# A pre-LN block of linear attention and spatial-gating MLP: earlier warm-up, head statistics on ScalarE, x loads held back, a split last tile, and a new instruction order

## The chip, the cores and the metric

One core of one Trainium2 chip. The metric is the device time of one execution in microseconds (us). Before the prediction the kernel had three unprofiled runs: median 236.93 us (236.36 to 237.14). PE is the tensor engine, VectorE is DVE in the profile, ScalarE is ACT, Pool is GpSimd, and SP is the engine that issues most of the DMAs.

## The reference, cut to what matters

Sequence S = 2048, width D = 512, half width Fh = 896, all in bf16.

```python
x = A_x
h  = x + _A_ref(_layernorm(x), A_wqkv, A_wo)                    # linear attention, 32 heads
h2 = h + _B_ref(_layernorm(h), B_w_in, B_w_sp, B_b_sp, B_w_out)

# _B_ref, cut:
z  = _gelu(x @ w_in)                       # 2048 x 1792
z1 = z[..., :Fh]
z2 = _layernorm(z[..., Fh:])
g  = einsum('ts,bsf->btf', w_sp, z2) + b_sp[None, :, None]   # mixes all 2048 rows
return (z1 * g) @ w_out
```

The mixer needs `w_sp` transposed on chip (2048 x 2048, 8 MB). It runs in two passes. Pass 0 computes row groups 0 and 2, pass 1 computes groups 1 and 3. The tile `wsp` in the chip's memory is filled with DMA transposes on SP's queue. Each group has a semaphore of its own (`wsp0` to `wsp3`), so a group counts as loaded when all of its parts have landed.

## The kernel before

The program is a list of operations (`add`), each with the engine it runs on and the tiles it reads and writes. A constant, `ORDER`, holds the sequence of all of them, from which each engine gets its own instruction list.

The loads of `wsp`. `order` lists the row tiles by need, those of pass 0 first. Tiles 2 to 7 of that list come in two halves, the others whole:

```python
order = [t for p in range(NG // 2) for tg in (p, p + NG // 2) for t in range(tg * TPG, (tg + 1) * TPG)]
for i, t in enumerate(order):
    w = NT // 2 if EARLY <= i < NT // 2 else NT
    for j in range(0, NT, w):
        dma_t(wsp[:, j:j + w, t * P:(t + 1) * P], B_w_sp[...], f"wsp{t // TPG}",
              issue=520 + 4 * w * 53.5).soft.add(...)      # landing: lat=1600
```

The first tiles, the last tile, and the warm-up (matmuls of zeros, meant to have PE at its full clock when the real work starts):

```python
pool(lambda p: p.memset(warm, 0.0), [], [warm], 100, bias=1e6)
...
warmup(48)
...
def k_unit(n):                        # two 128-row tiles of x
    for i in (n, n + 1):
        stats(x, 0, i)                # VectorE: bn_stats, bn_aggr
        if n == 0: rstd(...)          # Pool: (var + eps), then pow(-0.5)
    ...
        norm(...); pe_transposes(...) # VectorE, then PE, then ScalarE copies to xnT
    ... # matmuls with wqkv (k), phi (ScalarE Exp, VectorE twice), kv products

def mo(n, nb):                        # one output tile
    ... # 7 matmuls of 512 columns into a bank
    dve(lambda v: v.tensor_tensor(o, bank(b), h[:, n, :], ALU.add), ...)
    dma("SP", out_d[n * P:(n + 1) * P, :], o, f"o{n}", issue=600, lat=2000)
```

Of the kernel before, what the change touches and what calls it, by code (L numbers as in the profile page):

```python
# [15 lines left out]
ORDER = "c-jTQ1war05Cgz%k0L5!pjZfsf`}+8SQvny7zikW0d{wHcXxMpcXxMpcX#)lGhC1k8ITc~;D*e|f;P$yccg?PlEVQhU;qdq6>`7>X^<A_;fk#AL{8*_7jmO0d=Q9Y2tsj`Ks_X(K1!l4N}~!YAsh0*8+nlrzQ_+h1fw8Ip$y8xAC(b>02DwWG(bZ%Mk7>3G(r%H7*t0`v_~g&Kw-op4n@!mVQ7K~R6`BKBLPn6j4tSk?r4st=z;PmhlQwsa16&tj6hA)!YI^6YIH+S^g>HSq6I3V4ieD{^RWPn&>DNN7j3W)`!O10Fb>Hu7K^b2%div&a1e(u5#!MteXtUJ(GUHx9EULogE0g{F$|M10V}WyZP5->Fd4Hk3&$`OM=%EiFc8P_7)S945Ag);)Ikr>TGKEcb1@HVuo`Qz37atkGqDcqu?1VP4Lh(MCvgHhu?xF#3LCHyr*Q@sa2{uI1?O-PS8)lKaSbo<40rGxH*pKsaRX2B7ccP-js#QiHeTT^UgHZs<1U=|4sY-k_i!H{@g8aU13%$FBPo8sC!}L~{(>`8GZj-Z6EiR)U74KUkc{7vi!SuyZ=~TL1hO>!n1w;i&8#fSJoKgy^U|03S%%Rp&zh`2e->kLmS9O1U^bRz3^Q{hBN@Vi3}7e=(T%~Z$S{^;Ef!`2He@*SaT8mz6=T_n+3C(4^k6A=W=?vtH;1qfhcbdiSeu(!jg8oaTiBY7S)G+wnN8S~b=Zt?Y{Nt*u?7$EFo&@(hjRqSavYCvJmWc^fttnz3{n+#Wm|S*J9cLjCvYLRvM!Hu5f}3qSFj$Nb2?YDsEVrx`>{PcuqWFpfmPXp^;t|Mw1oXRfCD**BUw_VR9eBB!I_-MrQF5c3{e@aVp)ai6i+iu;VP#Hl~<%HsG=&ViYlwBq7<#c?8sgm#nBwYNu12p+{QCJ%RSu7Wt_rUoXzdr!8KgVIh@ONT+een&yL!_d0ft^j8UwrDNfZDuNtbU1l3k8C8~~+bcvT)Uv*Vaw|IrO`G}ACghkXt?bTJ?)k~e#MV-`51Jp<T)l+@dPrcPpuh>Yhd52edjZgWE*Lj!sc!T%(fH(PuZ@G{A`J4y%f}i-AU)VrR^^2z8OeF^;Q)>O;JO1TAKIB2Z<X2wcH@@cwCf9N9q@z;kJDv1{7wN1tN~sfc(Me`dGr20GGRaMul|>NMSlN_aUTUJ;`bl?vWDa@AQ)!h>Ih99}xBQe}{_;^?`Ko{lD!sBQpK>Wcg;ZFhHC!##TqCqli!@$KH9@VkOp~-i1GQaaG)Ut#SW~r1Q#4USv_m^JS-Uh=(=<v$wOAuHT`e?Qd$n9MG)F5nOmj6;v$R@kv|IDERvR^6OSDeEwLp7xK>M^_TeL}=wLu4UNQZSqTeVGRwO>bdO2>3sXLL@NbXn(hMaOkPS9M)CbW^u<LML@ccXdzq^-z!WSWom!&-Fqt^;&QARv+|HpOoJI=$~L2jF!>d%q*Gx&{zG`Fa6aw$-XPOxmpTKZBFK3j^=D>EVE^?l$OeJn~P<&Y?jtOE1hMs?3TlFS|0N;cYCK?=4Bq{Y5C00LaeBTS~2rAZ_97~me&ecuobaV7GdSBpaoixmA2wm!NRPJ1z4n&vl3Rw3R|2-TMdi17>l(^R@tgpHH)$Yd#a1Nrm_}p4^+}B+AF=+7ge|0s%kZ@mesa8mS{=#AF{cVy#"  # L16
# [236 lines left out]
def bass_sequential_preLN__linear_attn_block__mixer_gmlp__prompt_kernel(  # L253
# [214 lines left out]
    def first_load(eng, dst, src, nm, at):  # L468

        q = queue[eng]  # L470
        op = load(eng, dst, src, nm, at - 500.0 * (len(q) + 1))
# [4 lines left out]

    def load_x(eng, n, w, at):
        first_load(eng, x[:, n:n + w, :], x_d[n * P:(n + w) * P, :], f"x{n}", at)

# [217 lines left out]
    for tg in range(NG):  # L697
# [194 lines left out]
```

## Time and profile before

| | before |
|---|---|
| median of 3 unprofiled runs | 236.93 us |
| span of the profiled execution | 235.9 us (that execution took 237.73 us) |
| PE busy | 228.3 us, 97% |
| useful PE work (counted from groups by shape) | about 220.5 us |
| PE starts the mixer | 122.13 us |

From the page of before: engines' busy time, then the span in 40 slices with busy tenths (PEclk is the granted clock, DMA the engines' busy share).

```profile
span 235.9 us, 3066 instructions
...
PE 228.3 (97%) x1140; PEld 105.2 (45%) x1140; DVE 150.7 (64%) x278; ACT 92.4 (39%) x160; POOL 54.8 (23%) x155
...
PE   7799999999999998999999999999999999999994
...
PEclk9999999999999999999999999999999999999999
DMA  6963389926554336699999400000020000000044
```

PE is full everywhere but at the two ends, at full granted clock. So a change can only win at the ends and in small gaps. One caution on the PEclk row: the trace of before has no record of the clock ahead of 6.5 us, and the row counts such time as full. The warm-up matmuls start 107 ns apart until then and 56 ns apart afterwards, so the head ran at half clock although the row shows a 9.

PE in order of time, before (start, duration, what, count, and in brackets the idle time ahead of it and what ended it):

```profile
1.76 5.09 PE L567 MATMUL psum<-warm 128*128 128x128 bf16 x48 [1.76 <-POOL warm L439]
6.68 0.39 PE L547 MATMUL psum<-ident,xn 128*128 128x128 bf16 x4
...
11.19 1.90 PE L402 MATMUL psum<-wqkv,xnT 128*128 128x512 bf16 x8 [0.30 <-ACT xnT L421]
...
23.98 1.89 PE L402 MATMUL psum<-xnT,wqkv 128*128 128x512 bf16 x8
...
120.41 1.89 PE L402 MATMUL psum<-hnT,win 128*128 128x512 bf16 x8
122.13 10.66 PE L402 MATMUL psum<-wsp,z 128*128 128x512 bf16 x48
```

The lines are landmarks: warm-up, first transposes, tile 2's k projection, first q projection, last z1T projection, start of the mixer. The queue behind it, SP of before:

```profile
96.44 0.58 SPq L432 DMA_DIRECT2D bsp<-in_B_b_sp_dram  x1
97.06 33.27 SPq L435 DMA_TRANSPOSE wsp<-in_B_w_sp_dram  x16
```

The transposes go on until 130.3 us, 8 us after the mixer has started. That works because those issued last are for pass 1.

### The profile page before, as it was taken

The page shows a single profiled execution, that of the slowest core. Times are in us where ns is not written, and L with a number is a line of the kernel's source. Part 1 is how long each engine was busy: PE and PEld are TensorE (multiplying, and loading weights), DVE is VectorE, ACT ScalarE, POOL GpSimd, SP SyncE. Part 2 cuts the span into 40 slices and gives each one's busy share as a digit, 9 for nine tenths or more (in the row PEclk, how much of TensorE's full clock was granted, in tenths as well). Part 3 has the DMA queues.
Part 4 walks back from the last instruction along what each step waited for, and adds up shares of the span by engine and source line. Part 5 has one row for each costly group of instructions (what it writes and reads, how often), then busy time and mean ns, then how long its engine had stood idle before and what let it go on. Part 6 is the DMA issues. An engine that isn't in the chain of part 4 may idle for free.

```text
span 235.9 us, 3066 instructions
## 1 busy us (share of the span) xinstructions
PE 228.3 (97%) x1140; PEld 105.2 (45%) x1140; DVE 150.7 (64%) x278; ACT 92.4 (39%) x160; POOL 54.8 (23%) x155
## 2 busy tenths in 40 slices
PE   7799999999999998999999999999999999999994
PEld 7444444453334443445544444444444444444441
DVE  3899656659986452023899989786575055672464
ACT  2668653469689775678942010100001000100000
POOL 4454200000488883006881000000000000000000
PEclk9999999999999999999999999999999999999999
DMA  6963389926554336699999400000020000000044
GB/s 205 345 120 68 68 237 359 227 62 162 115 119 81 75 81 112 150 183 176 183 192 220 105 3 0 0 0 0 3 67 0 0 0 3 0 0 0 0 148 144
DMA packets 58686, 23.66 MB, mean 100 GB/s; under 512 B 48432, under 2 KB 58544, under 8 KB 58672
## 3 DMA queue, kind: packets, MB, share of 16 engines
q1 hardware_dynamic: 57840, 22.68, 43.4%
q10 hardware_dynamic: 832, 0.79, 1.0%
q8 instruction: 9, 0.15, 0.3%
q14 instruction: 5, 0.04, 0.1%
HBM read 7.47 MB, written 2.10 MB: 41 GB/s over the span
## 4 chain that ended last, share of the span: by engine, by line
PE 86%; DVE 5%; ACT 2%; POOL 2%; DMA 2%; issue 1%; ACTq 0%
PE psum L402 68%; PE psum L609 6%; PE psum L745 5%; PE psum L748 4%; DMA x<-in_A_x_dram 2%; DVE st L503 1%; DVE pqT L560 1%; ACT e L421 1%; DVE pqT L714 1%; POOL st L523 1%; POOL rs L528 1%; DVE h L726 1%; PE psum L674 0%; PE psum L630 0%; ACT m L421 0%
## 5 line engine op out<-in xcount | busy, mean ns | idle before, releaser
L402 PE MATMUL psum<-wsp,z 128*128 128x512 bf16 x208 | 47.1, 379 | 0.0
L421 ACT ACTIVATE psum<-psum 128x512 f32<-128x512 f32 x12 | 7.0, 582 | 87.6 <-DVE u L806 44.1
L402 PEld LDWEIGHTS psum<-wsp,z 128*128 128x128 bf16 x208 | 20.2, 98 | 24.8 <-DVE z L533 0.5
L402 PE MATMUL psum<-hnT,win 128*128 128x512 bf16 x112 | 25.8, 379 | 0.8 <-ACT z1T L421 0.8
L402 PE MATMUL psum<-wout,z1T 128*128 128x512 bf16 x112 | 25.3, 379 | 0.0
L806 DVE TENSOR_TENSOR u<-psum,bsp 128x512 bf16<-128x512 f32 x16 | 11.0, 690 | 20.7 <-PE psum L402 20.5
L402 PE MATMUL psum<-t,s 128*128 128x512 bf16 x96 | 21.9, 379 | 0.0
L421 ACT ACTIVATE e<-psum 128x1024 bf16<-128x1024 f32 (+1 forms) x18 | 16.7, 927 | 12.4 <-PE psum L402 12.1
L421 ACT ACTIVATE z1T<-psum 128x512 bf16<-128x512 f32 x28 | 16.4, 594 | 6.8 <-PE psum L402 6.5
L522 POOL TENSOR_SCALAR st<-st 128x1 f32<-128x1 f32 x23 | 5.5, 241 | 51.4 <-ACT sh L421 35.6
L402 PEld LDWEIGHTS psum<-wout,z1T 128*128 128x128 bf16 x112 | 11.0, 98 | 13.2 <-DVE z1T L807 0.5
L745 PE MATMUL psum<-win,hnT 128*128 128x512 bf16 x64 | 16.4, 379 | 0.0
L402 PEld LDWEIGHTS psum<-hnT,win 128*128 128x128 bf16 x112 | 9.9, 97 | 14.5 <-ACT z1T L421 5.1
L421 ACT ACTIVATE z<-psum 128x896 bf16<-128x896 f32 x16 | 14.6, 912 | 3.7 <-PE psum L748 3.6
L402 PE MATMUL psum<-m,pqT 128*128 128x512 bf16 x64 | 15.2, 380 | 0.5 <-DVE h L726 0.4
L402 PE MATMUL psum<-wqkv,xnT 128*128 128x512 bf16 x64 | 15.3, 379 | 0.3 <-ACT xnT L421 0.3
L797 DVE TENSOR_TENSOR h<-psum,h 128x512 bf16<-128x512 f32 x16 | 10.6, 687 | 7.7 <-PE psum L402 7.7
L609 PE MATMUL psum<-pk,xn 128*128 128x512 bf16 x64 | 15.5, 379 | 0.0
L761 DVE BATCH_NORM_STATS2 st<-z 128x6 f32<-128x512 bf16 x9 | 6.1, 683 | 14.6 <-ACT z L421 14.6
L402 PE MATMUL psum<-xnT,wqkv 128*128 128x512 bf16 x64 | 15.3, 379 | 0.0
L402 PEld LDWEIGHTS psum<-t,s 128*128 128x128 bf16 x96 | 9.4, 98 | 11.3
L503 DVE BATCH_NORM_STATS2 st<-x 128x6 f32<-128x512 bf16 x16 | 10.6, 682 | 4.4 <-DMA x<-in_A_x_dram 4.4
(87 smaller groups left out, 322.8 us busy)
## 6 DMA issues: line engine op xcount, KB each, us to landing
r<-rc SPq DMA_DIRECT2D x16, 128.0 KB, 2.6
out_dram<-h SPq DMA_DIRECT2D x16, 128.0 KB, 1.8
win<-in_B_w_in_dram SPq DMA_DIRECT2D x2, 896.0 KB, 5.4
x<-in_A_x_dram SPq DMA_DIRECT2D x5, 256.0 KB, 6.0
wqkv<-in_A_wqkv_dram SPq DMA_DIRECT2D x2, 512.0 KB, 6.0
wout<-in_B_w_out_dram SPq DMA_DIRECT2D x1, 896.0 KB, 8.6
wo<-in_A_wo_dram SPq DMA_DIRECT2D x1, 512.0 KB, 6.6
bsp<-in_B_b_sp_dram SPq DMA_DIRECT2D x1, 512.0 KB, 4.6
```

The lines of the kernel that those rows point to most:

```text
L402: inst = pe.matmul(out_ap, lhsT=a, rhs=b, start=start and i == 0, stop=stop and i == len(pairs) - 1, **kw)
L421: return g.add("ACT", lambda ac: ac.activation(out_ap, in_ap, func, **kw), [in_ap, *extra], [out_ap] + ([accum] if accum is not None else []),
L503: dve(lambda v: v.bn_stats(s[:, 0:6], src[:, n, :]), [src[:, n, :]], [s[:, 0:6]], D)
L522: pool(lambda p: p.tensor_scalar(mean, s[:, 0:1], 1.0 / n, None, op0=ALU.mult), [s[:, 0:1]], [mean], 190)
L523: pool(lambda p: p.tensor_scalar(s[:, 2:3], mean, mean, EPS_LN, op0=ALU.mult, op1=ALU.subtract), [mean], [s[:, 2:3]], 240)
L528: pool(lambda p: p.tensor_tensor(r, ve, expo[:, 0:1], ALU.pow), [ve, expo], [r], 620)
L609: inst = pe.matmul(bank(CB[c]), lhsT=xn[:, i, c * P:(c + 1) * P], rhs=pk[:, i, :], start=i == 0, stop=i == NT - 1)
L745: pe.matmul(bank(b), lhsT=hnT[:, c, n * P:(n + 1) * P], rhs=win2[:, c, 0:GW], start=c == 0, stop=c == KD - 1)
L748: inst = pe.matmul(bank(b + 1, F2), lhsT=hnT[:, c, n * P:(n + 1) * P], rhs=win2[:, c, GW:FH], start=c == 0, stop=c == KD - 1)
L761: dve(lambda v, n=n, s=s: v.bn_stats(s[:, 0:6], z2[:, n, 0:GW]), [z2[:, n, 0:GW]], [s[:, 0:6]], GW)
L797: dve(lambda v: v.tensor_tensor(o, bank(b), h[:, n, :], ALU.add), [bank(b), h[:, n, :]], [o], D, ps=True)
L806: dve(lambda v: v.tensor_tensor(t, bank(b), add, ALU.add), [bank(b), add], [t], GW, ps=True)
```

## The change

The intent: start the warm-up sooner, shorten the first statistics by using ScalarE for tiles 0 to 3, get tiles 2 and 3 of x in earlier, take VectorE off some critical evictions, and halve the last add and store. Every operation was put in a new order. The diff, cut to its core:

```diff
-ORDER = "c-jTQ1war05Cgz%k0L5!pjZfsf`}..."        (862 operations; cut)
+ORDER = "c-jrp1!D*b7zNOK?`LAeW@>6?!^GIc..."      (873 operations; cut)
...
+    g.ops[1].soft.add(0)                  # the warm memset goes first on Pool
...
-    load_x("SP", 4, 2, 6800)
-    load_x("ACT", 6, 2, 6800)
-    for n, t in ((8, 7600), (10, 8300), (12, 9100), (14, 9900)):
-        load_x("SP", n, 2, t)
+    for n, lat in ((4, 2400), (6, 2600), (8, 2800), (10, 3000), (12, 3200), (14, 3400)):
+        load_x("SP", n, 2, lat, x0)       # x0: wait for x0's landing
...
+    def rstd_act(s, r, n, w, col):
+        act_exp(rr[:, :, 1:2], ve, ACT.Ln, 80, bias=epst[:, 1:2], extra=[epst[:, 1:2]])
+        act_exp(rr[:, :, 0:1], rr[:, :, 1:2], ACT.Exp, 80, scale=-0.5)
...
     def phi(...):
+        if split:                         # the last two q units
+            act(dst, t, ACT.Identity, w * GW, bias=epst[:, 2:3], extra=[epst[:, 2:3]])
+            dve(lambda v: v.tensor_tensor(dst, dst, e, ALU.max), [dst, e], [dst], w * GW, acc=2)
...
-    warmup(48)
+    warmup(42)
...
+            if i in ACTS:                 # tile 1: sum and sum of squares on ScalarE, moments and pow on Pool
...
-                  issue=520 + 4 * w * 53.5).soft.add(queue["SP"][-1].i if i < EARLY else late.i)
+                  issue=3900 if i < EARLY else 1310 if w < NT else 2200).soft.add(...)
...
     def mo(n, nb):
+        w = D // 2 if n == NT - 1 else D   # last tile in two column halves, second stored from ACT
```

The line with `issue=` changes no instruction. It changes what the schedule believes a `wsp` transpose to cost: a half 1.31 instead of 2.23 us, a whole tile 2.2 instead of 3.94 us (only the first two tiles of the list, both of group 0, stay at 3.9).

More of the change, by code (lines that the diff above doesn't have):

```diff
@@ L15 @@
 SEM_NS = 45.0
-ORDER = "c-jTQ1war05Cgz%k0L5!pjZfsf`}+8SQvny7zikW0d{wHcXxMpcXxMpcX#)lGhC1k8ITc~;D*e|f;P$yccg?PlEVQhU;qdq6>`7>X^<A_;fk#AL{8*_7jmO0d=Q9Y2tsj`Ks_X(K1!l4N}~!YAsh0*8+nlrzQ_+h1fw8Ip$y8xAC(b>02DwWG(bZ%Mk7>3G(r%H7*t0`v_~g&Kw-op4n@!mVQ7K~R6`BKBLPn6j4tSk?r4st=z;PmhlQwsa16&tj6hA)!YI^6YIH+S^g>HSq6I3V4ieD{^RWPn&>DNN7j3W)`!O10Fb>Hu7K^b2%div&a1e(u5#!MteXtUJ(GUHx9EULogE0g{F$|M10V}WyZP5->Fd4Hk3&$`OM=%EiFc8P_7)S945Ag);)Ikr>TGKEcb1@HVuo`Qz37atkGqDcqu?1VP4Lh(MCvgHhu?xF#3LCHyr*Q@sa2{uI1?O-PS8)lKaSbo<40rGxH*pKsaRX2B7ccP-js#QiHeTT^UgHZs<1U=|4sY-k_i!H{@g8aU13%$FBPo8sC!}L~{(>`8GZj-Z6EiR)U74KUkc{7vi!SuyZ=~TL1hO>!n1w;i&8#fSJoKgy^U|03S%%Rp&zh`2e->kLmS9O1U^bRz3^Q{hBN@Vi3}7e=(T%~Z$S{^;Ef!`2He@*SaT8mz6=T_n+3C(4^k6A=W=?vtH;1qfhcbdiSeu(!jg8oaTiBY7S)G+wnN8S~b=Zt?Y{Nt*u?7$EFo&@(hjRqSavYCvJmWc^fttnz3{n+#Wm|S*J9cLjCvYLRvM!Hu5f}3qSFj$Nb2?YDsEVrx`>{PcuqWFpfmPXp^;t|Mw1oXRfCD**BUw_VR9eBB!I_-MrQF5c3{e@aVp)ai6i+iu;VP#Hl~<%HsG=&ViYlwBq7<#c?8sgm#nBwYNu12p+{QCJ%RSu7Wt_rUoXzdr!8KgVIh@ONT+een&yL!_d0ft^j8UwrDNfZDuNtbU1l3k8C8~~+bcvT)Uv*Vaw|IrO`G}ACghkXt?bTJ?)k~e#MV-`51Jp<T)l+@dPrcPpuh>Yhd52edjZgWE*Lj!sc!T%(fH(PuZ@G{A`J4y%f}i-AU)VrR^^2z8OeF^;Q)>O;JO1TAKIB2Z<X2wcH@@cwCf9N9q@z;kJDv1{7wN1tN~sfc(Me`dGr20GGRaMul|>NMSlN_aUTUJ;`bl?vWDa@AQ)!h>Ih99}xBQe}{_;^?`Ko{lD!sBQpK>Wcg;ZFhHC!##TqCqli!@$KH9@VkOp~-i1GQaaG)Ut#SW~r1Q#4USv_m^JS-Uh=(=<v$wOAuHT`e?Qd$n9MG)F5nOmj6;v$R@kv|IDERvR^6OSDeEwLp7xK>M^_TeL}=wLu4UNQZSqTeVGRwO>bdO2>3sXLL@NbXn(hMaOkPS9M)CbW^u<LML@ccXdzq^-z!WSWom!&-Fqt^;&QARv+|HpOoJI=$~L2jF!>d%q*Gx&{zG`Fa6aw$-XPOxmpTKZBFK3j^=D>EVE^?l$OeJn~P<&Y?jtOE1hMs?3TlFS|0N;cYCK?=4Bq{Y5C00LaeBTS~2rAZ_97~me&ecuobaV7GdSBpaoixmA2wm!NRPJ1z4n&vl3Rw3R|2-TMdi17>l(^R@tgpHH)$Yd#a1Nrm_}p4^+}B+AF=+7ge|0s%kZ@mesa8mS{=#AF{cVy#"
@@ new lines @@
+ORDER = "c-jrp1!D*b7zNOK?`LAeW@>6?!^GIc*f5Nx+SrDvF-&)NcXxMpcXxMpcX#vN`3=Vz>5v{7kqMdMhAha6YygN<NDW5_hGcMnJ95GWuE>Dw@Pr3)As@Vu8+ni%dEt!!ltLg%BN{o79|cet1yKe;@IhGwqZ%5aI-*br<xm0T;fIQ7j3Q`)MASeGnj#4)(G1N|6uu~i5QHKY#Ze3X2t!wNMmV~m3nCDQnrML%sEs;^M=M04F6v=4DxosQVjRYxJ{n*#mSPDGp(LuHDq5m7+Mq4EqX&AT7sg`(CSnqLqYwI`A10$663`I+F#yZZ9vyH12QeJO&=H+51<SDlY2bvzID!;dg_TH)shEa=7=)uZj$>Gh5g3e-7=`JWfz>#HQ<#Z)n2!Zmhc!5jr+9&r=&tAJrzhyBS(uH5ScD-MiuKrl?bwEm*o4j4ft}ceIhc#x*n=}Ti@n%~{n&!7xQr_}hx53Ai@1SHxQd&&hU>V6S9py#c!>wNjeEF@J4nX2a9|oHXIeV*J|5y7-s2;F;5$Cx6CU9)KI1F?;vX{cC%)h}zQK_xn3AcOp00FZIzIcqLT0)#JF_t>v+x(3n3{i(k@-j#VSbikMP^`8R$&2(rD+UdPR6kyeOQQv>C38gXH7O>Gv;7>`Z0k$Scb*u!Cb7yP}X7)i_@PaSdwKK#c~W|d4@BBwHe81#<LFVvN;3TklWdUE!m147|crS$vpI8ZhF$29odTmxr3vamxDN&quHB%Se-REn4LI=Q&^8vxsyZKntj=b{g}wcoW>@c!#0fJT+ZWsF5p5A<uDHCSWahWj^hl@<al;rS5Dwk2C_0Ma2=PiKi9J<+j0cEsy<_x#C9yD(ki2}3Q~EMQw0SpL>0AxyBMl4g=;wvFhY^4q{^zIYO1PeMX83WD@L(e#1&l0Rouu;+{`Up&57*BksQED?9RoU#jRY!CG4p|n$5M`#@_0sf$F5e>Y)MZrq1fGAsVVa>Y_mP)iBjmoNB4I;#EiWR96jDUkPfcgKVTko!|wYWMf_ADK=4(Ztww{>Lwquxti$~U+^Vc=mS6U6@Tz2f3dYFDU}?RPEKkgS7lLFWz!*E;$dFq6&~SLp5|_z;aOheIUeP09^)Rq=3egO9e(0xKH`49;amRZUB2TNnjZ5BuQQp>(?MVPjraJS$N7h;^_Ty6pYNGo8I)1U^_0)}oN1IoP)p^Kr&7vGxs_i<)Jg?ZRB4r6&T>&66_k&1$Xz*=SDBPqg;Y$%<tBd>mbZMBPag7936)fUCTfz#YOltrz1nK3R%@EtX^m!RorddxmTQGpX{APJvZiRHCTNy6Xq2XFw&rS~#%qrDX|(2Pt@dlC#^|u-Yk?MNv5sn^*6W~_XtS1TyS8YVHtCR#=$N)@hjwYFj%%Av=%hO6ly+;6PV0;=>w+%olCJ26ZtALT>8!5lw(jbl?(2ch>AW84v7YF;Ug)Ks>XqK;t={RqKI)S`>zlsohmxDj%)#6&g=H}(%Vs$&mHpN~{n1~gwloGyW@*jUQd(AXwx4pe^p?SBE|$*Rt$<}T56fjaEt6%pFUoAW&C|Th+X`AC%V+s5kL5K#D`I6V*n+Hr`C3u)v0@fxg{`;+TDVoVD&}vcthAN22&-xpEz+u4IV)i$Ex<x7!RlCDYiRYXk;Pe})wEhx+v;1iRks=zV@<57C0R3jrmy;?JNlsV_E4`CYEf3nt}EUeTLX)==Jp>gx|km"
@@ L442, in bass_sequential_preLN__linear_attn_block__mixer_gmlp__prompt_kernel @@
                                    channel_multiplier=1), [ident], [ident], 300, bias=1e6)
-    pool(lambda p: p.memset(epst[:, 0:1], EPS_DEN), [], [epst], 80, bias=1e6)
+    head = len(g.ops)
+    pool(lambda p: p.memset(epst[:, 0:1], EPS_DEN), [], [epst[:, 0:1]], 80, bias=1e6)
+    pool(lambda p: p.memset(epst[:, 1:2], EPS_LN), [], [epst[:, 1:2]], 80, bias=1e6)
+    pool(lambda p: p.memset(epst[:, 2:3], 1.0 + EPS_PHI), [], [epst[:, 2:3]], 80, bias=1e6)
     pool(lambda p: p.memset(expo, -0.5), [], [expo], 80, bias=1e6)
@@ L460, in bass_sequential_preLN__linear_attn_block__mixer_gmlp__prompt_kernel @@
                                    base=DH, channel_multiplier=-1), [selm], [selm], 300, bias=1e5)
+    g.ops[1].soft.add(0)
+    for op in g.ops[head:]:
+        op.soft.add(1)
     wq = A_wqkv.rearrange("(c p) f -> p c f", p=P)
@@ L466, in load, with first_load @@
         return dma(eng, dst, src.rearrange("(c p) f -> p c f", p=P), nm, lat=lat, issue=issue)
-    def first_load(eng, dst, src, nm, at):
+    def first_load(eng, dst, src, nm, lat, behind=None):
         q = queue[eng]
-        op = load(eng, dst, src, nm, at - 500.0 * (len(q) + 1))
+        op = load(eng, dst, src, nm, lat)
         op.bias = 1e6
@@ L474, in first_load, with load_x @@
             op.soft.add(q[-1].i)
+        if behind is not None:
+            op.deps.add(behind.i)
         q.append(op)
-    def load_x(eng, n, w, at):
-        first_load(eng, x[:, n:n + w, :], x_d[n * P:(n + w) * P, :], f"x{n}", at)
-    load_x("SP", 0, 1, 2650)
-    load_x("ACT", 1, 1, 2850)
-    for eng, c in (("SP", 0), ("ACT", 2)):
-        first_load(eng, wqkv[:, c:c + 2, D:2 * D], A_wqkv[c * P:(c + 2) * P, D:2 * D], f"wk{c}", 4800)
-    load_x("SP", 2, 1, 5300)
-    load_x("ACT", 3, 1, 5300)
-    load_x("SP", 4, 2, 6800)
-    load_x("ACT", 6, 2, 6800)
-    for n, t in ((8, 7600), (10, 8300), (12, 9100), (14, 9900)):
-        load_x("SP", n, 2, t)
-    first_load("SP", wqkv[:, :, 0:D], A_wqkv[:, 0:D], "wq", 11400)
+        return op
+    def load_x(eng, n, w, lat, behind=None):
+        return first_load(eng, x[:, n:n + w, :], x_d[n * P:(n + w) * P, :], f"x{n}", lat, behind)
+    x0 = load_x("SP", 0, 1, 2150)
+    load_x("ACT", 1, 1, 2350)
+    for eng, c in (("SP", 0), ("ACT", 2)):
+        first_load(eng, wqkv[:, c:c + 2, D:2 * D], A_wqkv[c * P:(c + 2) * P, D:2 * D], f"wk{c}", 3700)
+    load_x("SP", 2, 1, 3400)
+    load_x("ACT", 3, 1, 3400)
+    for n, lat in ((4, 2400), (6, 2600), (8, 2800), (10, 3000), (12, 3200), (14, 3400)):
+        load_x("SP", n, 2, lat, x0)
+    first_load("SP", wqkv[:, :, 0:D], A_wqkv[:, 0:D], "wq", 4600)
     exp_table = g.add("ACT", lambda ac: ac.preload_act_table_set("natural_log_exp_and_others"), [], [], cost=1300)
@@ L517, in rstd @@
                                                     op0=ALU.mult, op1=ALU.mult), [r[:, i, :], s[:, i, :]], [r[:, i, :]], 240)
+    def rstd_act(s, r, n, w, col):
+        rr, ve = r[:, n:n + w, :], s[:, n:n + w, col + 1:col + 2]
+        act_exp(rr[:, :, 1:2], ve, ACT.Ln, 80, bias=epst[:, 1:2], extra=[epst[:, 1:2]])
+        act_exp(rr[:, :, 0:1], rr[:, :, 1:2], ACT.Exp, 80, scale=-0.5)
     def moments(s, col, n):
         mean, ve = s[:, col:col + 1], s[:, col + 1:col + 2]
+        pool(lambda p: p.tensor_scalar(s[:, 2:3], s[:, 0:1], s[:, 0:1], -1.0 / (n * n), op0=ALU.mult, op1=ALU.mult), [s[:, 0:1]],
+             [s[:, 2:3]], 240)
+        pool(lambda p: p.tensor_scalar(ve, s[:, 2:3], s[:, 1:2], EPS_LN, op0=ALU.add, op1=ALU.add), [s[:, 1:3]], [ve], 240)
         pool(lambda p: p.tensor_scalar(mean, s[:, 0:1], 1.0 / n, None, op0=ALU.mult), [s[:, 0:1]], [mean], 190)
-        pool(lambda p: p.tensor_scalar(s[:, 2:3], mean, mean, EPS_LN, op0=ALU.mult, op1=ALU.subtract), [mean], [s[:, 2:3]],
-             240)
-        pool(lambda p: p.tensor_scalar(ve, s[:, 1:2], s[:, 2:3], None, op0=ALU.subtract), [s[:, 1:3]], [ve], 230)
     def rpow(ve, r):
@@ L552, in bass_sequential_preLN__linear_attn_block__mixer_gmlp__prompt_kernel, with phi @@
     ecnt = [0]
-    def phi(dst, b, w=2):
+    def phi(dst, b, w=2, split=False):
         e, t = e_t[ecnt[0] % NE][:, 0:w, :], psum[:, b:b + w, :]
@@ L559, in phi @@
         dve(lambda v: v.tensor_scalar(e, e, 1.0, EPS_PHI, op0=ALU.min, op1=ALU.add), [e], [e], w * GW, acc=4)
-        dve(lambda v: v.scalar_tensor_tensor(dst, t, 1.0 + EPS_PHI, e, op0=ALU.add, op1=ALU.max),
-            [t, e], [dst], w * GW, ps=True)
+        if split:
+            act(dst, t, ACT.Identity, w * GW, bias=epst[:, 2:3], extra=[epst[:, 2:3]])
+            dve(lambda v: v.tensor_tensor(dst, dst, e, ALU.max), [dst, e], [dst], w * GW, acc=2)
+        else:
+            dve(lambda v: v.scalar_tensor_tensor(dst, t, 1.0 + EPS_PHI, e, op0=ALU.add, op1=ALU.max),
+                [t, e], [dst], w * GW, ps=True)
     def warmup(n):
@@ L568, in fn @@
             return inst
-        PE(fn, [warm], [bank(7, P)], 2200 + n * 54, bias=1e6)
-    warmup(48)
+        PE(fn, [warm], [bank(7, P)], n * 103, bias=1e6)
+    warmup(42)
     PAIRS = [0, 2]
@@ L581, in bass_sequential_preLN__linear_attn_block__mixer_gmlp__prompt_kernel @@
     HEAD, SINGLE = 6, 4
+    ACTS = (1,)
+    QSPLIT, KSPLIT, CACT = (6, 7), (), 2
     def k_unit(n):
@@ L586, in k_unit @@
         for i in (n, n + 1):
-            stats(x, 0, i)
-            if n == 0:
-                rstd(st[0], rs[0], i, 1, 6, False)
-        if n:
+            if i in ACTS:
+                s = st[0][:, i, :]
+                act(sh_t[0], x[:, i, :], ACT.Identity, D, accum=s[:, 0:1])
+                act(sh_t[1], x[:, i, :], ACT.Square, D, scale=D ** -0.5, accum=s[:, 1:2])
+                moments(s, 6, D)
+                rpow(s[:, 7:8], rs[0][:, i, 0:1])
+            else:
+                stats(x, 0, i)
+                if n == 0:
+                    rstd_act(st[0], rs[0], i, 1, 6)
+        if n == 2:
+            rstd_act(st[0], rs[0], n, 2, 6)
+        elif n:
             rstd(st[0], rs[0], n, 2, 6, n >= HEAD)
@@ L603, in k_unit @@
         else:
-            phi(pk[:, n:n + 2, :], b)
+            phi(pk[:, n:n + 2, :], b, 2, n in KSPLIT)
         def fn(pe, i):
@@ L619, in q_unit @@
                                   for d in range(KD)])
-        phi(pqT[:, c:c + 2, tg * GW:(tg + 1) * GW], b)
+        phi(pqT[:, c:c + 2, tg * GW:(tg + 1) * GW], b, 2, 2 * tg + c // 2 in QSPLIT)
     def z_unit():
@@ L664, in bass_sequential_preLN__linear_attn_block__mixer_gmlp__prompt_kernel @@
     for c in range(KD):
-        if c % 2:
+        if c % 2 < CACT:
             act(ct[:, c, :], bank(CB[c]), ACT.Copy, GW)
@@ L707, in bass_sequential_preLN__linear_attn_block__mixer_gmlp__prompt_kernel @@
         PE(fn, [zc, pqT[:, :, tok]], [bank(db)], 450)
-        act_exp(r_t, bank(db), ACT.Ln, GW, bias=epst[:, 0:1], extra=[epst])
+        act_exp(r_t, bank(db), ACT.Ln, GW, bias=epst[:, 0:1], extra=[epst[:, 0:1]])
         act_exp(rc[tg % 2], r_t, ACT.Exp, GW, scale=-1.0)
@@ L784, in bass_sequential_preLN__linear_attn_block__mixer_gmlp__prompt_kernel @@
             dma_t(wsp[:, j:j + w, t * P:(t + 1) * P], B_w_sp[t * P:(t + 1) * P, j * P:(j + w) * P], f"wsp{t // TPG}",
-                  issue=520 + 4 * w * 53.5).soft.add(queue["SP"][-1].i if i < EARLY else late.i)
+                  issue=3900 if i < EARLY else 1310 if w < NT else 2200).soft.add(queue["SP"][-1].i if i < EARLY else late.i)
     EB, MB = [4, 5], [6, 7, 4, 5]
     def mo(n, nb):
-        b = MB[n % nb]
-        o = h[:, n, :]
-        parts = ((0, 3, 6, 1, 4), (2,), (5,))
-        for i, fcs in enumerate(parts):
-            matmuls(bank(b), [(z1T[:, fc, n * P:(n + 1) * P], wout[:, fc, :]) for fc in fcs],
-                    start=i == 0, stop=i == len(parts) - 1)
-        dve(lambda v: v.tensor_tensor(o, bank(b), h[:, n, :], ALU.add), [bank(b), h[:, n, :]], [o], D, ps=True)
-        dma("SP", out_d[n * P:(n + 1) * P, :], o, f"o{n}", issue=600, lat=2000)
-        g.final.append(f"o{n}")
+        w = D // 2 if n == NT - 1 else D
+        for j in range(0, D, w):
+            b, cs = MB[n % nb] if j == 0 else 0, slice(j, j + w)
+            o = h[:, n, cs]
+            parts = ((0, 3, 6, 1, 4), (2,), (5,))
+            for i, fcs in enumerate(parts):
+                matmuls(bank(b, w), [(z1T[:, fc, n * P:(n + 1) * P], wout[:, fc, cs]) for fc in fcs],
+                        start=i == 0, stop=i == len(parts) - 1)
+            dve(lambda v, o=o, b=b: v.tensor_tensor(o, bank(b, w), o, ALU.add), [bank(b, w), o], [o], w, ps=True)
+            dma("SP" if j == 0 else "ACT", out_d[n * P:(n + 1) * P, cs], o, f"o{n}{j}", issue=600, lat=2000)
+            g.final.append(f"o{n}{j}")
     cnt = [0, 0]
```

## The prediction

> **What bounds it now.** The tensor engine (PE): busy 228.3 of 235.9 us (page, busy times), and 86% of the chain that ended last. From 15.3 to 232.9 us the chain is almost all PE. Useful work, by the groups of shapes: 948 matmuls of 512 columns at 0.216 us, 64 of 384 at 0.162, and some 5.5 us of transposes and small products: about 220.5 us. The first transpose starts at 6.68 and the last matmul ends at about 232.95, so only about 6 us are idle behind the warm-up. Those, the 6.6 us ahead and the 2.9 us behind are all it can touch. By the timeline:
> - Head: x0 lands at 3.6; statistics and the Pool chain (0.19 + 0.56 us) and the norm end at 5.89, but the transposes wait until 6.63 for the 48 warm-up matmuls (start 1.76, 5.09 us, 106 ns each, so all at half clock, as the Trainium skill, "TensorE: Matmul & The Clock Gate", Part 1, gives for a cold array). x2 lands only at 6.67, and tile 2's projection starts at 11.19. PE idle between 6.63 and 15.3: about 2.1 us. VectorE is busy 8.63 of those 8.67.
> - Middle, 48 to 74 us: about 2.3 us of PE idle, behind VectorE's phi (1.23 us for one PSUM pass) and the Pool moments chain.
> - 91 us: 0.8 us, PE waiting for ScalarE's z1T.
> - Tail: VectorE 0.69 us and the store, 2.9 us.
>
> **What the change does.**
> 1. Warm memset first on Pool (now at 1.50, after: about 0.78): warm-up starts about 0.7 earlier; 42 x 0.106 = 4.45 us, ends about 5.5 instead of 6.85. The norm then releases tile 0's transposes.
> 2. rstd of tile 0 by Ln and Exp of one column: estimate from the skill's "ScalarE: Activation LUTs" (What ACT_TABLE_LOAD costs): 0.28 + 0.19 us, against 0.83 on Pool: 0.2 to 0.3 us less. No trace here shows that width. Tile 1's statistics go to ScalarE (0.6 + 0.19 us twice): 0.85 us off VectorE.
> 3. Holding x4 to x15 until x0 landed: ahead of x2 and x3 are then only x0, x1 and wk. By the DMA view 1.5 MB had moved by 6.8 us; the 1.0 MB needed is there about 1.1 us earlier: x2 lands near 5.5. Tile 0's projection starts near 6.5 (before 7.97), tile 2's near 9.5 to 10 (11.19). I carry 1.5 us through to the PE-bound stretch.
> 4. Middle: phi of the last two q units as ScalarE (about 1.0) plus a bf16 max on VectorE (about 0.65) instead of 1.23: 1.1 us less VectorE, 2 us more ScalarE; moments with the mean taken off the chain: 0.3 us less latency a tile; ct copies all on ScalarE: neutral. Together 0.6 us.
> 5. Gap at 91 us, by the new order: 0.2 us.
> 6. Tail: last add on 256 columns, about 0.4 for 0.69; store latency unchanged: 0.3 us.
>
> Sum: 1.5 + 0.6 + 0.2 + 0.3 = 2.6 us of 236.93: **234.3 us**, range 232.7 to 236.0. Chances: faster by over 2% (below 232.2) 0.06, within 2% 0.93, slower 0.01.
>
> **What would show it.** Warm-up starting before 1.2 and transposes before 5.8; x2's statistics before 5.8; tile 2's projection before 10.2; the last matmul near 230.5; the last VectorE add near 0.4 us.
>
> **What would make it wrong.** The clock: fewer warm-up matmuls, then a gap, could leave the first projections at half clock (1.7 us lost). VectorE, saturated until about 22 us, may give it back. ScalarE's extra work may become the new wait.

## More of the kernel before

Waits are worked out from reads and writes. A queue therefore runs strictly in the order that `ORDER` gives it, even if a later entry is needed sooner.

```python
ids = np.frombuffer(zlib.decompress(base64.b85decode(ORDER)), np.uint16).tolist()
...
    t = max([free[o.eng]] + [self.start[d] + self.ops[d].cost + self._lag(...) for d in o.deps | o.soft])
    self.start[i] = t                  # estimate from the costs written at each add()
    free[o.eng] = t + o.cost
...
self.order = {e: [o for o in self.seq if o.eng == e] for e in self.ENGS}
```

## The result

| | before | after |
|---|---|---|
| median | 236.77 us (6 runs) | 242.83 us (6 runs) |
| lowest to highest | 236.36 to 237.14 | 241.24 to 244.73 |
| span of the profiled execution | 235.9 us | 240.7 us |

The ratio of after to before is 1.0255, with a 95% interval from 1.0204 to 1.0306. Ratios here are the mean time of one kernel's runs over the mean of the other's of the same rounds, so they are not quite the ratio of the medians. Executions over 1.5% slower than the fastest of the same kernel are left out of the means. The change was slower by 2.5%. The prediction gave that a chance of 1 in 100.

From the page of after, the same rows:

```profile
span 240.7 us, 3080 instructions
...
PE 228.4 (95%) x1141; PEld 105.0 (44%) x1141; DVE 147.5 (61%) x275; ACT 97.6 (41%) x172; POOL 53.5 (22%) x155
...
PE   7799999999699999999929999999999999999995
...
PEclk9999999999999999999997999999999999999999
```

PE's busy time is the same to 0.1 us, so the 4.8 us between the spans show as idle time. (Two differences cancel in the busy time: the warm-up is 1.26 us shorter, and a stretch of the mixer, below, 1.55 us longer.) There is a 2 in slice 21, a 6 in slice 11, and a dip of the granted clock in slice 22. PE in order of time, after:

```profile
1.05 3.83 PE L583 MATMUL psum<-warm 128*128 128x128 bf16 x42 [1.05 <-POOL warm L439]
5.40 0.40 PE L559 MATMUL psum<-ident,xn 128*128 128x128 bf16 x4 [0.53 <-DVE xn L545]
...
9.46 2.76 PE L402 MATMUL psum<-wqkv,xnT 128*128 128x512 bf16 x12
...
23.10 1.89 PE L402 MATMUL psum<-xnT,wqkv 128*128 128x512 bf16 x8
...
66.04 2.76 PE L402 MATMUL psum<-m,pqT 128*128 128x512 bf16 x12 [1.86 <-DVE pqT L741]
...
119.63 1.89 PE L402 MATMUL psum<-hnT,win 128*128 128x512 bf16 x8
125.78 12.21 PE L402 MATMUL psum<-wsp,z 128*128 128x512 bf16 x48 [4.26 <-DMA wsp<-in_B_w_sp_dram]
```

The head did what was meant: the warm-up starts 0.71 us earlier, the first transposes come 1.28 us earlier, the first q projection 0.88 us earlier. At the last z1T projections PE is still 0.78 us ahead (119.63 against 120.41), in spite of a wait of 1.86 us at 64 us. Then it waits 4.26 us for `wsp`, and the 48 matmuls behind that take 12.21 us for the 10.66 of before. The chain of waits of after, in the same place (start, duration, what):

```profile
120.10 1.52 SPq L435
121.62 0.04 issue
121.66 3.98 DMA wsp<-in_B_w_sp_dram
125.64 0.14 issue
125.78 4.40 PE psum L402 x12
```

The chain runs through SP's queue: the last part of group 0 began to be issued at 121.66, and it landed at 125.64. The granted clock of after in two stretches (stretch, its length, PE busy and count, PEclk, DMA share, GB/s):

```profile
125.00:130.00 5.00, 4.22 (x13) 0.67 1.10 198
130.00:135.00 5.00, 5.00 (x24) 0.99 0.25 56
```

If the clock was either full or half, it was half for 2 x (0.33 + 0.01) x 5 = 3.4 us. The Trainium skill, "TensorE: Matmul & The Clock Gate", Part 1, says that an idle window of 4096 cycles of 1.2 GHz, 3.41 us, puts the array back to half rate. The trace agrees: 4.26 us of idle were followed by one such stretch, which costs about 3.4 / 2 = 1.7 us of work. That closes the sum of the two profiled executions: -0.78 (lead) + 4.26 (wait) + 1.7 (clock) - 0.4 (tail, experiment 6) = 4.8 us, as 240.7 - 235.9.

SP's queue, after:

```profile
94.57 28.61 SPq L435 DMA_TRANSPOSE wsp<-in_B_w_sp_dram  x14
123.63 0.35 SPq L432 DMA_DIRECT2D bsp<-in_B_b_sp_dram  x1
124.05 5.44 SPq L435 DMA_TRANSPOSE wsp<-in_B_w_sp_dram  x2
```

By volume this queue is not later than before's: the last of the same 22 transposes has been issued at 129.5 instead of 130.3 us. What differs is which ones come when. The two programs' lists, read from `ORDER` (first figure the group, h a half tile, W a whole one; groups 0 and 2 are needed for pass 0, 1 and 3 some 50 us later; | marks the load of `bsp`):

```
before  0W 0h 0h 0W 0h 2h | 2h 0h 2h 2h 1W 2h 2h 2h 2h 3W 1W 3W 1W 3W 3W 1W
after   2h 2h 0W 0h 2h 1W 2h 2h 1W 0W 3W 2h 1W 0h 0h 1W 3W 3W 2h 0h | 2h 3W
```

In before, all of pass 0 is ahead of seven of the eight whole tiles of pass 1. In after, the last half of group 0 is twentieth of 22, behind seven whole tiles of pass 1, and the last half of group 2 is twenty-first. This gives the theory: **the loss is the order of the `wsp` transposes on a queue that fills the DMA engines; the wait that follows also costs PE its clock.** The rivals: the volume comes too late as a whole (V), because no transpose goes out in the head any more; or the clock falls for a reason of its own (C).

### The profile page after: what moved, and what is told of

Read it like the earlier page. It is cut to its first block, busy times and chain, and to the rows that moved or that the text cites. A ratio compares the mean times of both kernels' runs of the same rounds, so it can differ in the third digit from the quotient of the medians.

```text
span 240.7 us, 3080 instructions
## 1 busy us (share of the span) xinstructions
PE 228.4 (95%) x1141; PEld 105.0 (44%) x1141; DVE 147.5 (61%) x275; ACT 97.6 (41%) x172; POOL 53.5 (22%) x155
## 4 chain that ended last, share of the span: by engine, by line
PE 63%; SPq 16%; DMA 5%; POOL 5%; ACT 4%; issue 2%; DVE 2%
PE psum L402 56%; SPq L435 15%; PE psum L636 6%; DMA r<-rc 2%; POOL rs L540 2%; DMA x<-in_A_x_dram 2%; DMA wsp<-in_B_w_sp_dram 2%; POOL st L534 1%; POOL st L536 1%; ACT ct L421 1%; ACT e L421 1%; POOL st L537 1%; ACT m L421 1%; DVE st L510 1%; SPq L722 1%
## 5 line engine op out<-in xcount | busy, mean ns | idle before, releaser
L402 PE MATMUL psum<-wsp,z 128*128 128x512 bf16 x208 | 48.7, 389 | 4.3 <-DMA wsp<-in_B_w_sp_dram 4.3
L402 PEld LDWEIGHTS psum<-wsp,z 128*128 128x128 bf16 x208 | 20.7, 100 | 30.3 <-issue 6.9
L402 PE MATMUL psum<-wout,z1T 128*128 128x512 bf16 (+1 forms) x119 | 25.3, 367 | 0.0
L402 PE MATMUL psum<-hnT,win 128*128 128x512 bf16 x112 | 25.3, 379 | 0.0
L402 PEld LDWEIGHTS psum<-wout,z1T 128*128 128x128 bf16 x119 | 11.6, 98 | 12.8 <-DVE z1T L836 0.5
L534 POOL TENSOR_SCALAR st<-st 128x1 f32<-128x1 f32 x24 | 7.5, 314 | 41.1 <-ACT sh L421 36.8
L402 PE MATMUL psum<-m,pqT 128*128 128x512 bf16 x64 | 14.5, 380 | 1.9 <-DVE pqT L741 1.9
L402 PE MATMUL psum<-xnT,wqkv 128*128 128x512 bf16 x64 | 15.3, 379 | 0.4 <-DVE pqT L576 0.4
L636 PE MATMUL psum<-pk,xn 128*128 128x512 bf16 x64 | 15.3, 379 | 0.0
L826 DVE TENSOR_TENSOR h<-psum,h 128x512 bf16<-128x512 f32 (+1 forms) x17 | 10.8, 656 | 6.9 <-PE psum L402 6.9
L540 POOL TENSOR_TENSOR rs<-st,expo 128x1 f32<-128x1 f32 x24 | 14.1, 591 | 1.1
```

What stands on the lines that cost most here:

```text
L402: inst = pe.matmul(out_ap, lhsT=a, rhs=b, start=start and i == 0, stop=stop and i == len(pairs) - 1, **kw)
L534: pool(lambda p: p.tensor_scalar(s[:, 2:3], s[:, 0:1], s[:, 0:1], -1.0 / (n * n), op0=ALU.mult, op1=ALU.mult), [s[:, 0:1]], [s[:, 2:3]], 240)
L540: pool(lambda p: p.tensor_tensor(r, ve, expo[:, 0:1], ALU.pow), [ve, expo], [r], 620)
L636: inst = pe.matmul(bank(CB[c]), lhsT=xn[:, i, c * P:(c + 1) * P], rhs=pk[:, i, :], start=i == 0, stop=i == NT - 1)
L826: dve(lambda v, o=o, b=b: v.tensor_tensor(o, bank(b, w), o, ALU.add), [bank(b, w), o], [o], w, ps=True)
```

## The experiments

All kernels gave correct results. "New order" below is the order of after.

**1. e1_sorted.** The kernel after; only the 22 transposes are exchanged among their own places on the queue.

```diff
-after  2h 2h 0W 0h 2h 1W 2h 2h 1W 0W 3W 2h 1W 0h 0h 1W 3W 3W 2h 0h | 2h 3W
+e1     0W 0W 0h 0h 0h 0h 2h 2h 2h 2h 2h 2h 2h 2h 1W 1W 1W 1W 3W 3W | 3W 3W
```

> The kernel after, with only the 22 wsp transposes on the sync engine's queue put in the order of need (both groups of the first mixer pass first), in the same slots. Theory Q (the loss is the queue's order: the last half of group wsp0, needed at 121.4 us, stands behind seven whole tiles that are needed 50 us later): the wait of 4.3 us for wsp goes, the clock stays at full, and the time is 236.8 - 0.8 (lead at 121 us) - 0.4 (tail) = 235.6 us, 234.8 to 236.2. Rival V (the volume: the transposes as a whole come too late, because none goes out in the head any more and the weight loads were moved): a wait of 2 us or more on wsp stays and the time is above 238. Rival C (the clock sinks by itself, whatever the wait): matmuls of the first mixer group stay slow, mean above 0.385 us, time about 237.2.

Measured: 236.76 us (before in the same rounds: 237.07), ratio 0.9992 (0.9961 to 1.0023). The wait for `wsp` is gone and the clock stays full. PE in order of time, e1_sorted:

```profile
120.20 3.62 PE L402 MATMUL psum<-wsp,z 128*128 128x512 bf16 x16
124.91 1.47 PE L402 MATMUL psum<-wsp,z 128*128 128x512 bf16 x6 [1.09 <-DVE z L545]
```

So one reordering of DMAs took back the 6 us; V and C fall. But the time is 1.2 us above the 235.6 that the theory gave, and the second line says where part of it went. In the place of the wait for `wsp` there is now one of 1.09 us for the norm of the last z2 tile, which had been hidden under it.

**2. e2_before_mixed.** The reverse: the kernel before, with only its transposes behind the first one put in the sequence of after.

```diff
-before 0W 0h 0h 0W 0h 2h | 2h 0h 2h 2h 1W 2h 2h 2h 2h 3W 1W 3W 1W 3W 3W 1W
+e2     0W 2h 2h 0W 0h 2h | 1W 2h 2h 1W 3W 2h 1W 0h 0h 1W 3W 3W 2h 0h 2h 3W
```

> The kernel before, with only the wsp transposes behind the first one put in the mixed order of the kernel after, in before's own slots; everything else is as before. Theory Q: the last half of wsp0 is the third last to be issued, near 125 us, and lands near 129, so that PE waits 5 to 8 us near 122 us and runs part of the next group at half clock: 243 to 247 us. Rival V: before's slots hold the same volume in the same time, so the time stays at 236.8 plus or minus 1.

Measured: 247.12 us against 237.07, ratio 1.0415 (1.0380 to 1.0451), a shade above the expected range. What PE waited for (us in total, times, longest), and then the granted clock in three stretches of this run:

```profile
PE psum L402 <- DMA wsp<-in_B_w_sp_dram: 7.8, 1, 7.8
```

```profile
120.00:125.00 5.00, 1.77 (x9) 0.97 1.13 238
125.00:130.00 5.00, 0.41 (x2) 0.50 0.99 189
130.00:135.00 5.00, 5.00 (x13) 0.51 0.51 105
```

The order alone makes a good kernel 4% slower: 7.8 us of wait. Half clock for 2 x (0.03 + 0.50 + 0.49) x 5 = 10.2 us, three windows of 3.41, of which PE worked at half clock from 129.6 to about 134.9, at a cost of 2.6 us. Together 10.4, measured 10.05. The cause is shown from both sides. The clock goes with the wait: all ten runs of after and of this kernel show a mean granted clock of 0.993 or less, against 1 of the 33 runs of before that were timed beside the experiments.

**3. e3_sorted_win2.** What of the wait of 1.86 us at 64 us in after? It waits for `pqT`, and that for a copy of `r` that took 4.67 us to land, against a median of 2.7. One suspect was the load of `win2`, which the new order puts among these copies.

```diff
 e1_sorted: SP
   ... win1, wsp, wv, wsp, r (8 copies),
-  win2,
   r (8 copies) ...
+  (win2 directly behind wv)
```

> e1_sorted with the load of win2 moved from its place between the r copies (55.5 us) to just behind wv (about 38 us). Theory M: the PE wait of 1.9 us near 64 us (for pqT, which waits for an r copy that took 4.7 us) comes from win2's 0.9 MB running ahead of the r copies in the same DMA engines; then the r copies land in 2 to 3 us, the wait shrinks to under 0.8, and the time is 1.0 to 1.5 us below e1_sorted: about 234.4. Rival D: the wait at 64 us is set by the VectorE and ScalarE chain (phi split, moments), not by the copy: the wait stays over 1.4 us and the time is within 0.4 of e1_sorted.

Measured: 236.70 us, ratio 0.9988 (0.9956 to 1.0020), 0.06 below e1_sorted. But in e1_sorted, with `win2` in the suspected place, that wait was already only 0.27 us, as here. There was nothing left to save, and theory M got no support. In experiment 8 the wait is back (1.7 us, a copy of 4.3 us) with `win2` moved away. So `win2` does not explain it. It showed in two traces (after and e8_nohold2), both of the new order, and its cause is open.

**4. e4_sorted_nohold.** e1_sorted, with the later x loads no longer held back.

```diff
-        load_x("SP", n, 2, lat, x0)
+        load_x("SP", n, 2, lat)
```

> e1_sorted with the x loads no longer held back behind x0 (same order of issue). If holding back is what brings x2 in early: x2's statistics start near 6.6 instead of 5.9 us, and the time is 0.3 to 0.7 us above e1_sorted. If it was the order of issue alone (x4 and x6 behind x2 and x3, x6 off the scalar queue): x2 at 5.9 or earlier and the time within 0.3.

Measured: 237.96 us as median of six, ratio 1.0014 (0.9979 to 1.0049). The profiled run was an outlier of 617.87 us: the 512-column matmuls took about 836 ns instead of 379. Its granted clock is given as 1.0, but its trace has no record of the clock at all (its page lacks the PEclk row), so that figure says nothing. Nothing is concluded from its trace, and the experiment was repeated as e8.

**5. e5_zfirst.** Is the new wait of 1.1 us for the last z2 tile a matter of PE's order?

```diff
 e3_sorted_win2: PE, last projections (Z = z2 tile, . = z1T group), and ScalarE's evictions alike
-  ... ZZZ . ZZZZ . ZZZ ..
+  ... ZZZ ZZZZ ZZZ ....
```

> e3_sorted_win2 with two z1T projections (2 x 0.86 us of PE) moved behind the last z2 projection, on PE and ScalarE, so that the last z2 tile is projected 1.7 us earlier. Theory Z (with the queue in order, the next thing that the early start runs into is the 6.4 us from the last z2 projection to its norm, a wait of 1.1 us at 123.7 us, which hides most of the lead): the wait shrinks to under 0.4 us and the time is 0.7 to 1.1 us below e3_sorted_win2, about 235.8. Rival: VectorE and Pool, nearly full at that point, set the time of the last norm, not PE: the wait stays near 1 us and the time within 0.4 us of e3_sorted_win2.

Measured: 236.81 us (before: 236.71), ratio 0.9985 (0.9957 to 1.0012), no better than e3. The wait halved, without any gain in time (e5_zfirst):

```profile
125.39 4.91 PE L402 MATMUL psum<-wsp,z 128*128 128x512 bf16 x21 [0.53 <-DVE z L545]
```

The last z2 projection ended at 117.79 us, 0.7 us earlier than in e1_sorted (118.47), yet the norm of that tile ended at 125.24 instead of 124.85. This trace is a late one: no record of full clock comes before 10.4 us, its first projections start 0.40 to 0.43 us apart instead of 0.22, and the first q projection comes at 23.63 us, against 22.97 in e3. Read against that start, the projection came more than 1 us earlier than in e1 and the norm 0.1. The wait halved because PE came later (the mixer starts at 121.25, in e3 at 120.04), not because the tile came earlier. PE's order does not set it. The rival holds: it is set by what VectorE and Pool still have queued.

**6. e6_before_tail.** The kernel before, with only the last output tile split.

```diff
+        w = D // 2 if n == NT - 1 else D
+        for j in range(0, D, w):
+            b, cs = MB[n % nb] if j == 0 else 0, slice(j, j + w)
             ...
-        dma("SP", out_d[n * P:(n + 1) * P, :], o, ...)
+            dma("SP" if j == 0 else "ACT", out_d[n * P:(n + 1) * P, cs], o, ...)
```

> The kernel before, with only the last output tile in two column halves (the second one stored from the scalar queue). The predicted term was 0.3 us: last VectorE add 0.42 for 0.69 us; 0.2 to 0.4 us faster than before. Also a second trace of before's program up to 228 us: if the gap of 0.8 us at 91 us in the first trace of before was chance, it isn't there, and the mixer starts near 121.4 in place of 122.1.

Measured: 236.32 us against 236.71, ratio 0.9972 (0.9946 to 0.9998). This term of the prediction was right in size (0.3 predicted, 0.4 by medians). From the last matmul to the end of the span it is 2.56 us here and 2.95 in before. This is the only kernel whose interval lies below 1, by a hair; as one of eleven intervals that alone would prove little. It is also a second trace of before's program up to 228 us:

```profile
120.83 10.64 PE L402 MATMUL psum<-wsp,z 128*128 128x512 bf16 x47
```

The mixer starts at 120.83, not 122.13: the gap of 0.8 us at 91 us is not there (nor is it in e2 or e7, of the same program but for one edit), and the head is 0.3 us earlier. The one trace of before that the prediction was built on was a late one.

**7. e7_before_warm.** The kernel before, with only the warm memset first and 42 warm-up matmuls.

```diff
-    warmup(48)
+    warmup(42)
     ORDER: operation 0 (the warm memset) moved to the front
```

> The kernel before, with only the warm memset first on Pool and 42 in place of 48 warm-up matmuls. The first transposes come at about 5.95 (released by the norm) in place of 6.68. If VectorE and the landing of x2 set the head, as the prediction's risk says, tile 2's projection stays at 11.2 and the time within 0.3 us of before; if the warm-up was what held it, tile 2 comes 0.7 earlier and the time is 0.5 to 0.7 us lower.

Measured: 237.31 us against 236.71, ratio 1.0025 (0.9986 to 1.0065). PE in order of time, e7_before_warm:

```profile
5.82 0.40 PE L547 MATMUL psum<-ident,xn 128*128 128x128 bf16 x4
7.44 0.40 PE L547 MATMUL psum<-ident,xn 128*128 128x128 bf16 x4 [1.22 <-DVE xn L533]
...
11.08 1.90 PE L402 MATMUL psum<-wqkv,xnT 128*128 128x512 bf16 x8 [0.30 <-ACT xnT L421]
```

The transposes came at 5.82, and tile 2's projection still came at 11.08. The warm-up was not what held the head. Its three runs at a mean clock of 0.998 or more took 236.6 to 236.9 us; the three others, 237.7 to 239.4 us, show 0.986 or 0.993. A window of 3.41 us at half clock takes about 0.007 from the mean, so those had one or two. Where in those runs they fell can't be seen without a trace.

**8. e8_nohold2.** e3_sorted_win2 without the hold on the x loads (the edit of e4).

> e3_sorted_win2 with the x loads not held back behind x0 (the earlier try of this fell into an execution with PE at a third of its speed and left no usable profile). x2's statistics start near 6.5 in place of 5.8 us, and the time is 0.3 to 1.0 us above e3_sorted_win2; if holding back does nothing, within 0.2.

Measured: 236.74 us against 236.71, ratio 0.9993 (0.9967 to 1.0018), against 0.9988 and 0.9992 with the hold: no difference. VectorE in order of time, e8_nohold2:

```profile
5.71 1.29 DVE L510 BATCH_NORM_STATS2 st<-x 128x6 f32<-128x512 bf16 x2 [0.36 <-DMA x<-in_A_x_dram]
```

x2's statistics start at 5.71 without the hold, and at 5.92, 5.75 and 5.79 with it (after, e1, e3). Holding back did nothing. x2 comes earlier than in before (6.67) in all four, so the new order of issue is enough for it.

**9. e9_tile15_act.** e3_sorted_win2, with the statistics of the last z2 tile on ScalarE, and its Pool chain and norm ahead of tile 14's.

```diff
-        if n % 2 == 0 and n < NT - 2:
+        if n % 2 == 0 and n < NT - 2 or n == NT - 1:
             gl = act(z2[:, n, :], src, ACT.Gelu_apprx_tanh, FH, accum=s[:, 0:1])
             act(sq_t, z2[:, n, :], ACT.Square, FH, scale=FH ** -0.5, accum=s[:, 1:2])
```

> e3_sorted_win2 with the statistics of the last z2 tile taken by ScalarE (which idles there) in place of VectorE: 1.45 us less on VectorE between 118 and 124.5 us. Theory V2 (after e5_zfirst: the wait of 1.1 us in the first mixer group is set by VectorE, whose statistics and norms of the last three z2 tiles queue up, not by PE's order): the wait falls under 0.3 us, and the time is 0.7 to 1.0 us below e3_sorted_win2, about 235.8, ratio to before about 0.995. Rival: the Pool chain (pow) sets it, then the wait stays over 0.8 us and the ratio at 0.9985 or above.

Measured: 237.30 us against 236.73, ratio 1.0018 (0.9992 to 1.0045). The wait only fell from 1.1 to 0.86 us. VectorE in order of time, e9_tile15_act:

```profile
123.14 0.51 DVE L545 TENSOR_SCALAR z<-z,st,rs 128x896 bf16<-128x896 bf16 x1 [1.18 <-POOL rs L540]
124.10 0.51 DVE L545 TENSOR_SCALAR z<-z,st,rs 128x896 bf16<-128x896 bf16 x1 [0.44 <-POOL rs L518]
```

VectorE now idles, and waits for Pool. The theory that VectorE alone set it falls: Pool's chains stand right behind VectorE, and the last norm ended at 124.61 us, hardly earlier than in e1_sorted. Even what it gained can't be put down to the edit: two operations on Pool near 113 us were faster in this trace than in e1's, as in that of experiment 10.

**10. e10_tile1_dve.** e3_sorted_win2, with tile 1's statistics back on VectorE, and its rstd by Ln and Exp.

```diff
-    ACTS = (1,)
+    ACTS = ()
     ORDER: tile 1's bn_stats, bn_aggr, Ln, Exp and its norm directly behind tile 0's
```

> e3_sorted_win2 with tile 1's statistics back on VectorE and its rstd by Ln and Exp as tile 0's (no ScalarE pass, no Pool chain for it). If taking 0.85 us off VectorE in the head carries to the end, as the prediction has it: the first q projection (near 23.0 us) comes 0.5 to 0.9 us later and the time is 0.4 to 0.8 us higher. Rival: VectorE idles there anyway until x2 lands (0.6 us before the first norm, 0.3 after), so the same work fits into that idle time: the first q projection within 0.3 us of 23.0 and the time within 0.3 us of e3_sorted_win2.

Measured: 236.46 us against 236.73, ratio 0.9994 (0.9971 to 1.0016). The first q projection starts at 23.38 us, against 22.97 in e3_sorted_win2 and 23.13 in e1_sorted: 0.25 to 0.41 us later, and the time no higher. What VectorE was relieved of had fitted into its idle time, for the most part.

In this trace the wait for the last z2 tile is almost gone (0.15 us), and two operations on Pool show where that comes from, first in e1_sorted, then in e10_tile1_dve:

```profile
112.60 0.70 POOL L534 TENSOR_SCALAR st<-st 128x1 f32<-128x1 f32 x1
113.37 0.77 POOL L537 TENSOR_SCALAR st<-st 128x1 f32<-128x1 f32 x1
```

```profile
112.85 0.36 POOL L534 TENSOR_SCALAR st<-st 128x1 f32<-128x1 f32 x1
113.28 0.31 POOL L537 TENSOR_SCALAR st<-st 128x1 f32<-128x1 f32 x1
```

Up to there VectorE and Pool run 0.25 us behind e1's times. After it the same operations in the same order come 0.7 us earlier than in e1, VectorE's two waits for Pool (0.43 and 0.45 us near 116 and 117 us) are gone but for 0.07, and the last norm ends at 124.16 instead of 124.85. So, between these two traces, it is Pool's chain near 113 us that moves the end of the last norm. In e3, e5 and e8 the two took 0.70 and 0.77 us as in e1, in e9 0.36 and 0.31 as here. Why they are slow or fast is open.

## Why the prediction was wrong

The prediction was 234.3 us with a range from 232.7 to 236.0; measured were 242.83. Point by point:

1. **The step that failed** is one that the text made in half a sentence, "Gap at 91 us, by the new order: 0.2 us", together with the sum, in which no term stood for what the order could cost. From 15.3 us on the prediction had PE alone on the path. The new order was taken as harmless. The prediction priced what was added and removed, and did not ask what the new order does to a queue that is already full. In before's profile this could be seen: DMA engines at 9 tenths from 100 to 130 us, transposes on the queue past the start of the mixer. In its place the runs showed a wait of 4.26 us for `wsp` and one window of half clock. Undoing the order of the transposes alone took the 6 us away (experiment 1), and imposing it on before cost 10 (experiment 2).
2. **"What would make the prediction wrong"** named the clock, VectorE and ScalarE. The clock did fall, but in the mixer and behind a DMA wait. The risk that it did name, a head at half clock, shows in one trace of the new order (e5, 0.7 us late at the first q projection), not in that of after. A wait for a DMA was not among the risks.
3. **Why the queue was put so** is argued, not shown. The diff changes the believed cost of a transpose. The program works out its own estimate (`self.start`) as it is built, and this can be read without a run. For after it has the 14 transposes begin at 91.3 us and take 7 x 1.31 + 6 x 2.2 + 3.9 = 26.3 us; the last half of group 0 lands at 119.1, where PE starts the mixer. On the chip they began at 94.57, took 28.6 us (the estimate was 8% too low), and the last landed 2.5 us behind its issue instead of 1.6: 125.64, which is 6.5 us late, while PE itself came only 2.3 us late. To this estimate the order was free: it gives 232.9 us for after and 233.0 for e1's sorted order. With the old costs in the same program it gives 251.3 us, which leaves no room for such an order. A second thing made the wait long: the estimate lets a matmul wait for the parts it reads, but all parts of a group share a semaphore. By the program, the first 16 matmuls of the mixer (3.5 us) read only parts of group 0 that had landed by 114.9 us in after's trace; they waited for a part that the seventeenth reads first. With a semaphore for each part the wait would by this trace have been an estimated 0.8 us. No run tested that.
4. **Head (predicted 1.5).** The mechanism was right and the size was not. The first q projection of the new order starts on average at 23.19 us (after, e1, e3, e5, e9), that of before's program at 24.02 (before, e2, e6): 0.83 us. (Without e5, whose head was at half clock until 10.4 us, and the late trace of before, it is 1.0.) Of its parts, the warm-up gave nothing by itself (e7), the hold gave nothing (e8), and the ScalarE statistics of tile 1 gave at most 0.4 us at this point and nothing in the time (e10). Tile 0's Ln and Exp took 0.29 + 0.20 us, as estimated from the skill's "ScalarE: Activation LUTs", What ACT_TABLE_LOAD costs (0.28 + 0.19). What of the 0.83 us is due to them and what to the order of loads was not separated. Of the six signs that the prediction named, three came in after: the warm-up (1.05), the transposes (5.40) and the last add (0.42); x2's statistics (5.92) and tile 2's projection (10.3) just missed, the last matmul (238.2) did not come near.
5. **Middle and the gap at 91 us (predicted 0.8).** With the queue in order, PE reaches the mixer at 120.42 on average (e1, e3, e5, e9), before's program at 121.53 (before, e2, e6): a lead of 1.1 us. By these averages 0.3 of it is from the middle, but most of that is chance. From the first q projection to the mixer it is 97.07 or 97.08 us in e1, e3 and e9 and 97.18 in e2 and e6, which gives 0.1 us for the middle; before's one trace had the gap at 91 us, which is chance (experiment 6), so there was nothing to win there. The split phi did what was costed (VectorE 0.69 for 1.22 us, ScalarE 1.1 more).
6. **The lead is not paid out.** PE then waits 0.5 to 1.1 us (mean 0.9 in these four traces) for the last z2 tile. In before's traces PE arrives just as that tile is ready: in e6's, the seventeenth matmul of the mixer, the first that reads it, starts at 124.39, and the last norm ends at 124.33. The prediction treated the stretch from 15.3 us on as bound by PE alone, because the chain of waits showed only PE there. A second chain (VectorE and Pool) ran alongside with no slack, and in the new order it ended no earlier (124.16 to 125.43 in all its traces, 124.33 to 125.65 in before's program), although PE did.
7. **Tail (predicted 0.3): right.** The last add took 0.42 for 0.69 us, and e6 measured 0.4 us, in the median and in the trace.

With the queue in order, then, 1.1 - 0.9 + 0.4 = 0.6 us of the predicted 2.6 are left by the traces, and the timed runs show about 0.1% in e1, e3 and e5 and nothing in e9, which their intervals do not separate from zero. The best kernel is before with the split last tile alone: 236.32 us, ratio 0.9972.

## What to carry to other kernels

When a change brings a new order, check each full queue for what is needed first: list its entries, mark when each is needed, and see how many entries of later need stand ahead of it. A schedule computed from cost constants is as good as the constants of its busiest queue; let them err on the high side there, and sort by need wherever the order is free. Where parts of a tile share a semaphore, the part that lands last sets the start. And when the chain of waits shows one engine alone, look for the chain right behind it before counting a lead as a gain.

## What the Trainium skill lacked or had wrong

- "DMA: Bandwidth & Descriptors", Latency and other measured facts, gives 261 GB/s as the effective bandwidth of a DMA transpose with a non-contiguous middle dimension (measured on one kernel), and 350 to 400 for a contiguous one. Here a queue of transposes from DRAM, with the DMA engines full (share 0.95 to 1.09), moved 172 to 202 GB/s between 100 and 118 us in after. A transpose took 3.4 to 8.3 us from issue to landing, median 5.1.
- "TensorE: Matmul & The Clock Gate", Part 1, has the window of 3.41 us, and the traces agree: 3.4 us at half clock after 4.26 us of idle, and 10.2 us, three windows, around an idle stretch of 7.8 us. The page names a profile's total of throttled time; it does not say how the mean granted clock of a run, which is all that a run without a trace leaves here, shows the windows: each takes 0.007 from it in a run of 240 us, so that 0.993 and 0.986 are one and two. Three runs of after at 0.993 averaged 241.76 us, three at 0.986 averaged 243.84. The half clock of the head isn't in this figure: in before it reads 1.00 up to 6.63 us, with warm-up matmuls 107 ns apart.
- No page that I read explains an execution like the one of 617.87 us, in which 512-column matmuls took 836 ns instead of 379 from start to end. The clock-gate page comes near: it warns that its trace events can be unreliable, and reports a clock gate stuck at a quarter for more than 50 us. Whether this was such a case can't be told, since the trace has no record of the clock. It came once, and its cause is open.
